# Gram-matrix transfers on GpSimd's queue from the fifth chunk on, and a later first input for the second layer

## The chip, the cores and the metric

The kernel runs on one core of a Trainium2 chip. The metric is the device time of one execution in microseconds (us). The kernel before takes 1139.2 us, the median of three runs (1139.18, 1139.20 and 1141.53).

## What is computed

A delta-rule attention over 4 batches, 8 heads, 768 steps and head size 48, whose output goes through two feed-forward layers with 3072 tokens, model width 384 and inner width 2048, all in float32:

```
for t in range(768):
    y[:, :, t] = q[t] @ state
    v_old = state^T @ k[t]                      # k normalised
    state += beta[t] * outer(k[t], v[t] - v_old)
x  = y as 3072 tokens x 384
h  = x @ w_in;   x = (max(h, 0) + alpha * min(h, 0)) @ w_out     # layer 1
h  = max(x @ w_in2, 0);   out = (h * h) @ w_out2                 # layer 2
```

## The kernel before

The delta rule is cut into 12 chunks of 64 steps (`NCH`), and each chunk into two units u = 2c and 2c + 1 of eight (batch, head) groups of 128 partitions. A chunk needs the inverse of a triangular matrix that is built from the chunk's Gram matrix (keys times keys). This early part does not depend on the state, so it runs well ahead of the steps that carry the state on:

- `early(u)` has three pieces. `keys` normalises the keys, `transp` transposes them, and `gram` (L346) multiplies them. TensorE leaves the Gram matrix in PSUM; ScalarE copies its diagonal blocks into the tile `gs` and they are stored to `gscr` (L355); the off-diagonal blocks go to the tile `go` in two f16 parts and are stored to `oscr` (L362). With a chunk's second unit the matrix is read back from `gscr` in another layout by four loads into the tile `prob` (L370): two for each half of the partitions, one of whole rows and one of the right half of the lower rows.
- `inverse(k)` works on a pair of chunks, 2k and 2k + 1. VectorE scales `prob` (L391) and eliminates column by column (L397, L398). At its end, `fin` writes the result back over `prob` in two f16 parts and stores it to `tscr` with four stores (L406). There is one `prob` buffer, so the next pair's `prob` loads wait for these stores. I call the time between one pair's last column and the next pair's first a handover.
- `both` and `steps` are the chunk's steps. They load the inverse from `tscr` into `diag` (L422) and the off-diagonal blocks from `oscr` into `cross` (L430), and multiply with them. Keys come back through `kbd` and `ktb` (L472, L478), queries and values through `qr` and `vr` (L259, L261). The output y goes to HBM, to `x1d` (L528); for most chunks it stands in the buffer `t` of the weight pool on its way.

The feed-forward layers run beside this. Layer 1 takes a tile of 256 tokens for each chunk, layer 2 a tile of 512 tokens, and each tile passes 16 blocks j of the inner width. Every product is three matmuls with values split into a high and a low part in float32r. For a block, `emit_h` makes the first product (L632, nine matmuls), ScalarE and VectorE the nonlinearity (L110 and L639 in layer 1, L641 and L642 in layer 2) and the split of the result into `gh` (L644, ScalarE) and `gl` (L645, VectorE); `emit_acc` makes the second product (L664, nine matmuls), three blocks behind in layer 1. After a tile's last block, ScalarE copies the sums of layer 1 into a buffer of the tag `xf` (L673), and they are stored to `x2d` (L675).

`load_x(n)` loads a tile's input into `xf`, and `take_x(n)` splits it: ScalarE casts it into `xh` (L569), VectorE subtracts to get `xl` (L570). Tiles n = 0 to 11 belong to layer 1, n = 12 to 17 to layer 2. A tile of layer 2 is made of two halves of 256 tokens, from two tiles of layer 1, one in `xf` of the pool `moe` (the same single buffer that L673 writes) and one in `xf` of the pool `w2p[0]`. That pool opens where the delta rule's pools close. In it, `load_w1` loads raw weights of layer 2 (L725, GpSimd's queue, three `raw` buffers), and VectorE turns them into high and low parts, twice for each block (L589 to L592, L734, L736).

What sets the order: the program puts each piece into a list at a time t, in units of a block of layer 1 (`at`, L219), and that time, less an `ahead`, becomes the priority of its instructions (`urgency`). A planner then runs the program in a model of its own, gives each engine, among the instructions that it reckons ready, the one of highest priority, and so writes each engine's order once and for all. On the chip every engine works in that order and waits where an operand is late. Transfers are issued by SyncE (SP in the profile; it does nothing else) or by GpSimd (POOL). SP has the Gram transfers, `tscr`, `diag`, `cross`, `x1d`, `xf` and `x2d`; POOL has keys, queries, values, `kscr`, `fscr`, `kbd`, `ktb`, `bt` and most raw weights. `tc.issue_after(i)` keeps the instructions under it behind the instruction i.

Of the kernel before, what the change touches and what calls it, by code (L numbers as in the profile page):

```python
# [9 lines left out]
F32 = mybir.dt.float32  # L10
# [11 lines left out]
DM, DFF = 384, 2048  # L22
CH = 64
NCH = S // CH
# [54 lines left out]
CHAIN = 4  # L79
EARLY = 3  # L80
INV = 15
WQ = 8
UR = 7
WN = 11
# [6 lines left out]
def kernel(ctx: ExitStack, tc: tile.TileContext, qT, ktok, vtok, beta, w1, w2, alpha, cmask, hmask, eye, ident, out):  # L91
# [205 lines left out]
    def early(u):  # L297
        c, s = divmod(u, 2)
        d = {}

        def keys():
            kn = kts[c][:, 8 * s:8 * s + 8]
            rb = nr[c][:, 8 * s:8 * s + 8].unsqueeze(2).to_broadcast([128, NG, D])
            (G if c > NV else V).tensor_tensor(out=kn, in0=kn, in1=rb, op=ALU.mult)
            if u == 3:
                d["loan"] = loan(2).bitcast(F16)
            kh = d["loan"][:, 0:2 * DM].rearrange("p (t g e) -> p t g e", t=2, g=NG) if u == 3 else new(erl, [128, 2, NG, D], F16, "kh") if c else uhs[s]
            split(kh, kn, 1.0, G if c in KP else V)
            d["ktb"] = d["loan"][:, 2 * DM:2 * DM + 2 * NG * HD].rearrange("p (t g e) -> p t g e", t=2, g=NG) if u == 3 else new(erl, [128, 2, NG, HD], F16, "ktbE") if c else new(stp, [128, 2, NG, HD], F16, "ktb", KB)
            spread(d["ktb"], kh, tmask, c < SPK)  # L310
            if c:
                G.dma_start(out=kscr[u], in_=d["ktb"])

        def transp():
            ktb = d["ktb"]
            if u == 3:
                t = loan(1).bitcast(F16)[0:HD]
                kbd = [t[:, 1024 * i:1024 * i + 1024].rearrange("p (g i) -> p g i", g=NG) for i in range(2)]
                kf = t[:, 2048:3072].rearrange("p (t g i) -> p t g i", t=2, g=NG)
            else:  # L320
                whole = new(erl, [HD, 2, NG, 128], F16, "kbdE") if c else new(stp, [HD, 2, NG, 128], F16, "kbd", 2)
                kbd = [whole[:, i] for i in range(2)]
                kf = new(erl, [HD, 2, NG, CH], F16, "kf") if c else new(stp, [HD, 2, NG, CH], F16, "qh", 2)
            d["kbd"] = kbd
            for i in range(2):
                ps = bank(128, CH, ebank(c))
                for g in range(NG):
                    w = wide(ktb, i, g)
                    nc.tensor.matmul(ps[0:w.shape[1], g], lhsT=w, rhs=i2, start=True, stop=True)
                ps = ps[0:HD]  # L330
                scaled(kf[:, i], ps)
                for h in range(2):
                    o, k = heads(kbd[i])[:, :, :, h], ps.rearrange("p g (b i) -> p g b i", b=2)
                    if c > EV or h:
                        scaled(o, k, fmask[h])
                    else:
                        V.tensor_scalar(out=o, in0=k, scalar1=fmask[h], scalar2=None, op0=ALU.mult)
            if c == 0:
                kept[u] = whole, d["ktb"]
            elif u == 3:  # L340
                for i in range(2):
                    G.dma_start(out=fscr[u][:, i], in_=kbd[i])
            else:
                G.dma_start(out=fscr[u], in_=whole)
            d["kf"] = kf

        def gram():
            ps = bank(tag=ebank(c))
            for g in range(NG):
                for n, (i, j) in enumerate(((0, 0), (0, 1), (1, 0))):  # L350
                    nc.tensor.matmul(ps[:, g], lhsT=d["kbd"][i][:, g], rhs=d["kf"][:, j, g], start=n == 0, stop=n == 2)  # L351
            gs = new(stp, [128, NG, CH], F32, "pf")[:, :, 0:32] if u > UR else new(moe, [128, TOK], F32, "r1", R1).rearrange("p (g i) -> p g i", g=NG)
            for b in range(2):
                scaled(gs[64 * b:64 * b + 64], ps[64 * b:64 * b + 64, :, 32 * b:32 * b + 32])
            nc.sync.dma_start(out=gscr[c][s].rearrange("g j i -> j g i"), in_=gs)  # L355
            half = first(0, s)
            if c < 2:
                go = (d["loan"][:, 2304:2816] if u == 3 else gos[:, 512 * u:512 * u + 512]).rearrange("p (g i t) -> p g i t", i=32, t=2)[half]
            else:
                go = new(erl, [128, NG, 32, 2], F16, "go")[half]  # L360
            split(go.rearrange("p g i t -> p t g i"), ps[half, :, 32 * (1 - s):32 * (1 - s) + 32], 1.0)
            nc.sync.dma_start(out=oscr[u], in_=go)  # L362
            if u % 4 == 0:
                bts[c // 2] = new(erl, [128, 2, 32], F32, "bt")
                G.dma_start(out=bts[c // 2], in_=beta[c:c + 2].rearrange("c p i -> p c i"))
            if s:
                rows = gscr[c].rearrange("s g (q j) i -> (s g q) j i", q=4)
                for e in range(2):
                    for h, a in enumerate(halves(prob)):
                        i = nc.sync.dma_start(out=a[64 * e:64 * e + 64, c % 2], in_=rows[:, 16 * h:16 * h + 16, 16 * h:])  # L370
                        probs[c] = i.ins

        return keys, transp, gram
# [5 lines left out]
    def inverse(k):  # L379

        a, x, bt = prob, inv, bts[k]
        ops = []

        def init():
            G.memset(x, 0.0)
            for e in range(2):
                scaled(x.rearrange("p c a b -> p c (a b)")[64 * e:64 * e + 64, :, e:512:34], bt[64 * e:64 * e + 64, :, e::2], 256.0)
            for h, t in enumerate(halves(a)):
                for c in range(2):
                    b = bt[:, c, 16 * h:].unsqueeze(1).to_broadcast([128, 16, 32 - 16 * h])  # L390
                    V.scalar_tensor_tensor(out=t[:, c], in0=t[:, c], scalar=0.00390625, in1=b, op0=ALU.mult, op1=ALU.mult)  # L391

        def col(j):
            m, n = j // 2 + 1, 31 - j
            t = new(erl, [128, 272], F32, "col")[:, :2 * m * n].rearrange("p (c a b) -> p c a b", c=2, a=m)
            row = halves(a)[j // 16][:, :, j % 16:j % 16 + 1, j % 16 + 1:].to_broadcast([128, 2, m, n])
            V.tensor_tensor(out=t, in0=row, in1=x[:, :, 0:m, j:j + 1].to_broadcast([128, 2, m, n]), op=ALU.mult)  # L397
            i = V.tensor_tensor(out=x[:, :, 0:m, j + 1:], in0=x[:, :, 0:m, j + 1:], in1=t, op=ALU.subtract)  # L398
            columns.setdefault(k, []).append(i.ins)

        def fin():
            for c in range(2):
                t = a[:, c, 0:512].bitcast(F16).rearrange("p (m i t) -> p m i t", m=16, t=2)
                split(t.rearrange("p m i t -> p t m i"), x[:, c], 1.0)
                for e in range(2):
                    nc.sync.dma_start(out=tscr[2 * k + c][:, e::2], in_=t[64 * e:64 * e + 64])  # L406

        ops.append(init)
        for j in range(31):
            ops.append(lambda j=j: col(j))  # L410
        ops.append(fin)
        return ops

# [137 lines left out]
    def load_x(n):  # L551

        if n < NCH:
            xf[n] = [new(moe, [128, KD, TOK], F32, "xf")]
            nc.sync.dma_start(out=xf[n][0][0:HD], in_=x1d[n][:, 0:KD])
            nc.sync.dma_start(out=xf[n][0][HD:128], in_=x1d[n][:, KD].rearrange("(m p) i -> p m i", m=KD))
        else:
            xf[n] = [new(moe, [128, KD, TOK], F32, "xf"), new(w2p[0], [128, KD, TOK], F32, "xf")]
            for h, t in enumerate(xf[n]):
                nc.sync.dma_start(out=t, in_=x2d[n - NCH][:, :, h])  # L560

    def take_x(n):
        src = xf.pop(n)
# [2 lines left out]
        for m, (xh, xl) in enumerate(xs[n]):  # L566
            for h, t in enumerate(src):
                cols = slice(TOK * h, TOK * h + TOK)
                A.copy(out=xh[:, cols], in_=t[:, m])  # L569
                (G if m in TG and n < NCH else V).tensor_tensor(out=xl[:, cols], in0=t[:, m], in1=xh[:, cols].bitcast(F32), op=ALU.subtract)  # L570


# [45 lines left out]
            A.copy(out=wl[i], in_=ps[i])  # L618


    gt, acc = {}, {}

    def emit_h(layer, t, j):
        wh, wl = (t[0] for t in wt[layer, j])
# [16 lines left out]
            A.activation(out=g, in_=ps, func=ACTF.Relu)  # L641
            A.activation(out=g, in_=g, func=ACTF.Square)  # L642
        gh, gl = (new(p, [128, w], F32R, n, LAGB + 1 if layer else GB) for n in ("gh", "gl"))
        A.copy(out=gh, in_=g)  # L644
        (V if layer or j not in GP else G).tensor_tensor(out=gl, in0=g, in1=gh.bitcast(F32), op=ALU.subtract)  # L645
        gt[layer, t, j] = gh, gl

# [62 lines left out]
    for n in range(NCH + NCH // 2):  # L710
        t = 16 * n if n < NCH else 32 * n - 16 * NCH
        at(t - 5, load_x, n)
        at(t + TT, take_x, n)
    for j in range(NF):
        at(W0T + j, load_w0, j, ahead=AW)
    end = 16 * NCH
# [120 lines left out]
```

## Time and profile before

| | |
|---|---|
| median of 3 runs | 1139.2 us |
| the profiled execution | 1140.61 us |
| its span, first to last instruction | 1138.8 us |
| TensorE matmuls busy | 1054.2 us, 93% of the span |
| VectorE, ScalarE busy | 736.5 us, 728.6 us |
| GpSimd busy | 118.7 us, 206 instructions |
| granted TensorE clock, mean | 0.975 |

All times are microseconds from the span's start, on the one core. PE is TensorE, DVE VectorE, ACT ScalarE, POOL GpSimd and SP SyncE; an engine's name with a q is its sequencer, which issues transfers. "Busy" does not count the time in which an engine waits. The granted clock is the share of TensorE's full rate (2.4 GHz) that it was allowed in a stretch; a stretch at half the rate shows as 0.5, and a mean between 0.5 and 1 is a mix of both.

### The profile page before, as it was taken

What the parts mean: (1) busy time and instruction counts of PE and PEld (TensorE: products, weight loads), DVE (VectorE), ACT (ScalarE), POOL (GpSimd) and SP (SyncE); (2) the same over time, 40 slices, a digit from 0 to 9 for tenths busy, and PEclk for the clock granted to TensorE, in tenths of its full rate; (3) what the DMA queues carried; (4) which work ended last, traced back from release to release, by engine and by line L of the source; (5) the groups of instructions that cost most, each with busy time, mean ns of one, the idle gap of its engine ahead of it and who ended that gap; (6) DMA issues with size and microseconds to landing.
All of it is one profiled execution on the core that took longest, in us unless ns stands there. A gap on an engine that the chain in (4) does not pass through costs nothing.

```text
span 1138.8 us, 25230 instructions
## 1 busy us (share of the span) xinstructions
PE 1054.2 (93%) x9952; PEld 935.1 (82%) x9952; DVE 736.5 (65%) x1904; ACT 728.6 (64%) x1583; POOL 118.7 (10%) x206
## 2 busy tenths in 40 slices
PE   2766889899999979999999989999999999999997
PEld 2434579899999979999999989988888888888886
DVE  6998789699789869988986759888312121221211
ACT  7867678777767866885566546577645454454543
POOL 5111111111111111110110001011000000000000
PEclk9988899999999989999999989999999999999999
DMA  9585457545545464464353143343101000010000
GB/s 307 121 297 124 108 138 183 128 138 138 136 115 150 137 156 114 131 164 112 80 136 87 46 131 98 94 141 109 56 1 56 0 28 28 1 56 1 28 1 28
DMA packets 162886, 116.78 MB, mean 103 GB/s; under 512 B 122032, under 2 KB 143536, under 8 KB 162768
## 3 DMA queue, kind: packets, MB, share of 16 engines
q0 software_dynamic: 16320, 67.45, 19.3%
q1 hardware_dynamic: 146448, 47.73, 17.6%
q8 instruction: 78, 1.28, 0.5%
q14 instruction: 40, 0.33, 0.1%
HBM read 75.82 MB, written 39.32 MB: 101 GB/s over the span
## 4 chain that ended last, share of the span: by engine, by line
PE 73%; issue 8%; DMA 7%; DVE 6%; ACT 4%; SPq 1%; POOL 1%; POOLq 0%; ACTq 0%; DVEq 0%
PE h L632 32%; PE acc L664 31%; PE pa L133 3%; PE pa L123 3%; PE h L612 1%; DMA prob<-gscr 1%; DMA xf<-x2d 1%; PE h L613 1%; DMA xf<-x1d 1%; DMA al<-in_alpha_dram 1%; DMA gscr<-pf 1%; DMA vr<-in_vtok_dram 1%; ACT kbdE L110 1%; PE pe L351 0%; DVE w L590 0%
## 5 line engine op out<-in xcount | busy, mean ns | idle before, releaser
L632 PE MATMUL h<-xh,w 128*128 128x256 f32 (+1 forms) x1728 | 440.1, 325 | 4.7 <-DVE r L639 3.2
L664 PE MATMUL acc<-gh,w 128*128 128x256 f32 (+1 forms) x1728 | 431.8, 323 | 6.8 <-ACT xf L673 5.5
L632 PEld LDWEIGHTS h<-xh,w 128*128 128x128 f32 x1728 | 304.2, 192 | 29.8 <-DVE r L639 4.5
L645 DVE TENSOR_TENSOR gl<-r,gh 128x256 fp32r<-128x256 f32 (+1 forms) x288 | 145.4, 507 | 277.8 <-ACT gh L644 277.5
L664 PEld LDWEIGHTS acc<-gh,w 128*128 128x128 f32 x1728 | 299.1, 192 | 30.4 <-ACT xf L673 6.3
L632 PE MATMUL h<-xl,w 128*128 128x256 f32 (+1 forms) x864 | 278.5, 322 | 0.0
L664 PE MATMUL acc<-gl,w 128*128 128x256 f32 (+1 forms) x864 | 275.2, 322 | 3.6 <-DVE gl L645 3.4
L664 PEld LDWEIGHTS acc<-gl,w 128*128 128x128 f32 x864 | 165.2, 191 | 16.5 <-DVE gl L645 4.7
L632 PEld LDWEIGHTS h<-xl,w 128*128 128x128 f32 x864 | 166.2, 192 | 11.1
L644 ACT CAST gh<-r 128x256 fp32r<-128x256 f32 (+1 forms) x288 | 136.0, 476 | 52.9 <-DVE r L639 44.9
L641 ACT ACTIVATE r<-h 128x512 f32<-128x512 f32 x96 | 57.1, 596 | 148.0 <-PE h L632 141.2
L110 ACT ACTIVATE r<-h,sgn 128x256 f32<-128x256 f32 x192 | 89.9, 472 | 61.8 <-PE h L632 56.4
L639 DVE SCALAR_TENSOR_TENSOR r<-h,bet,r 128x256 f32<-128x256 f32 x192 | 90.9, 476 | 20.8 <-ACT r L110 19.9
L398 DVE TENSOR_TENSOR inv<-inv,col 128x252 f32<-128x252 f32 (+22 forms) x186 | 63.8, 343 | 1.7
L397 DVE TENSOR_TENSOR col<-prob,inv 128x252 f32<-128x252 f32 (+22 forms) x186 | 63.5, 341 | 1.5
L642 ACT ACTIVATE r<-r 128x512 f32<-128x512 f32 x96 | 60.7, 633 | 2.6
L123 PEld LDWEIGHTS <-kbd 96*128 96x128 f16 x1104 | 38.7, 99 | 7.7 <-issue 3.2
L612 PE MATMUL h<-w,idf 128*128 128x384 f32 x64 | 35.8, 648 | 7.3 <-ACT w L618 7.3
L133 PE MATMUL pa<-ph,ubd 128*128 128x64 f16 (+1 forms) x576 | 38.7, 194 | 0.9 <-ACT ubd L110 0.9
L569 ACT CAST xh<-xf 128x256 fp32r<-128x256 f32 x72 | 25.3, 403 | 20.0 <-DMA xf<-x2d 8.5
L570 DVE TENSOR_TENSOR xl<-xf,xh 128x256 fp32r<-128x256 f32 x72 | 26.6, 420 | 15.1 <-ACT xh L569 15.1
L133 PE MATMUL pa<-qh,sbd 96*128 96x64 f16 (+1 forms) x528 | 35.3, 194 | 0.0
(176 smaller groups left out, 1392.0 us busy)
## 6 DMA issues: line engine op xcount, KB each, us to landing
raw<-in_w_dram POOLq DMA_DIRECT2D x32, 384.0 KB, 3.4
kbd<-fscr POOLq DMA_DIRECT2D x22, 384.0 KB, 4.2
ktb<-kscr POOLq DMA_DIRECT2D x22, 384.0 KB, 3.6
kscr<-ktbE POOLq DMA_DIRECT2D x21, 384.0 KB, 3.4
fscr<-kbdE POOLq DMA_DIRECT2D x21, 384.0 KB, 3.4
w<-in_w_dram POOLq DMA_DIRECT2D x8, 768.0 KB, 9.2
w<-in_w_dram SPq DMA_DIRECT2D x8, 768.0 KB, 12.2
vr<-in_vtok_dram POOLq DMA_DIRECT2D x24, 192.0 KB, 4.1
```

Source lines behind the costliest of these rows:

```text
L110: A.activation(out=out, in_=in_, func=ACTF.Copy if isinstance(scale, float) else ACTF.Identity, scale=scale)
L123: nc.tensor.matmul(ps, lhsT=w[:, i], rhs=x[:, j], start=start and n == 0, stop=stop and n == 2)
L133: nc.tensor.matmul(ps[0:w.shape[1], g], lhsT=w, rhs=x[:, j, g], start=start and n == 0, stop=stop and n == 2)
L397: V.tensor_tensor(out=t, in0=row, in1=x[:, :, 0:m, j:j + 1].to_broadcast([128, 2, m, n]), op=ALU.mult)
L398: i = V.tensor_tensor(out=x[:, :, 0:m, j + 1:], in0=x[:, :, 0:m, j + 1:], in1=t, op=ALU.subtract)
L632: nc.tensor.matmul(ps, lhsT=a[:, sl], rhs=x, start=(n == 0), stop=(n == 8))
L639: V.scalar_tensor_tensor(out=g, in0=ps, scalar=bet[:, j:j + 1], in1=g, op0=ALU.mult, op1=ALU.max)
L641: A.activation(out=g, in_=ps, func=ACTF.Relu)
L642: A.activation(out=g, in_=g, func=ACTF.Square)
L644: A.copy(out=gh, in_=g)
L645: (V if layer or j not in GP else G).tensor_tensor(out=gl, in0=g, in1=gh.bitcast(F32), op=ALU.subtract)
L664: i = nc.tensor.matmul(acc[m], lhsT=a[:, sl], rhs=g, start=(j == 0 and n == 0 and (layer == 1 or m != 1)), stop=(j == NF - 1 and n == 2), ...
```

## The change

The four kinds of Gram transfers, and the two loads of the second layer's first input (n = 12), get a choice of queue. With `GD = "gop"` and `QG = 3` the stores to `gscr` ("g") and `oscr` ("o") and the loads of `prob` ("p") are issued by GpSimd for chunks c > 3; the stores to `tscr` ("t") stay on SyncE. With `XG = 1` both halves of input 12 are loaded by GpSimd. Its first half no longer uses `xf` of `moe` but the weight pool's buffer `t`. Its cast is put into the list at t - 0.6 instead of t - 3, and each cast is held behind the cast of `gh` of block 14 (`NF - 2`) of layer 1's last tile. Inputs 13 to 17 are as before.

```
+XG = 1
+GD = "gop"
+QG = 3
...
-            nc.sync.dma_start(out=gscr[c][s].rearrange("g j i -> j g i"), in_=gs)
+            (G if c > QG and "g" in GD else nc.sync).dma_start(out=gscr[c][s].rearrange("g j i -> j g i"), in_=gs)
...
-            nc.sync.dma_start(out=oscr[u], in_=go)
+            (G if c > QG and "o" in GD else nc.sync).dma_start(out=oscr[u], in_=go)
...
-                        i = nc.sync.dma_start(out=a[64 * e:64 * e + 64, c % 2], in_=rows[:, 16 * h:16 * h + 16, 16 * h:])
+                        i = (G if c > QG and "p" in GD else nc.sync).dma_start(out=a[64 * e:64 * e + 64, c % 2], in_=rows[:, 16 * h:16 * h + 16, 16 * h:])
...
-                    nc.sync.dma_start(out=tscr[2 * k + c][:, e::2], in_=t[64 * e:64 * e + 64])
+                    (G if 2 * k > QG and "t" in GD else nc.sync).dma_start(out=tscr[2 * k + c][:, e::2], in_=t[64 * e:64 * e + 64])
...
-            xf[n] = [new(moe, [128, KD, TOK], F32, "xf"), new(w2p[0], [128, KD, TOK], F32, "xf")]
+            one = new(wpool, [128, 2 * DM], F32, "t", TB).rearrange("p (m i) -> p m i", m=KD) if n == NCH else new(moe, [128, KD, TOK], F32, "xf")
+            xf[n] = [one, new(w2p[0], [128, KD, TOK], F32, "xf")]
             for h, t in enumerate(xf[n]):
-                nc.sync.dma_start(out=t, in_=x2d[n - NCH][:, :, h])
+                (G if n == NCH and XG else nc.sync).dma_start(out=t, in_=x2d[n - NCH][:, :, h])
...
-                A.copy(out=xh[:, cols], in_=t[:, m])
+                with tc.issue_after(last[NF - 2]) if n == NCH else nullcontext():
+                    A.copy(out=xh[:, cols], in_=t[:, m])
...
-        A.copy(out=gh, in_=g)
+        i = A.copy(out=gh, in_=g)
+        if (layer, t) == (0, NCH - 1):
+            last[j] = i.ins
...
-        at(t + TT, take_x, n)
+        at(t + (TT if n != NCH else -0.6), take_x, n)
```

## Rows read from the trace of the kernel before

**Rows 1.** The page, part 1: busy us, share of span, instructions.

```profile
PE 1054.2 (93%) x9952; PEld 935.1 (82%) x9952; DVE 736.5 (65%) x1904; ACT 728.6 (64%) x1583; POOL 118.7 (10%) x206
```

**Rows 2.** Busy by long stretches: length, busy by engine, clock, DMA share, GB/s.

```profile
160.00:600.00 440.00, 422.14 (x5922) 411.21 (x5919) 377.59 (x1085) 320.60 (x762) 66.44 (x116) 0.99 0.54 136
...
800.00:1128.00 328.00, 328.00 (x1449) 271.60 (x1448) 66.86 (x112) 165.55 (x288) 0.00 (x0) 1.00 0.06 22
```

**Rows 3.** Busy by stretches of 20 us, same columns (PE PEld DVE ACT POOL).

```profile
400.00:420.00 20.00, 13.50 (x155) 12.36 (x154) 11.55 (x24) 11.52 (x27) 2.99 (x5) 0.85 0.72 156
...
660.00:680.00 20.00, 16.11 (x116) 15.90 (x115) 10.19 (x26) 9.28 (x25) 2.13 (x4) 0.83 0.47 149
...
700.00:720.00 20.00, 17.54 (x133) 16.88 (x132) 16.79 (x44) 11.60 (x30) 1.83 (x4) 0.94 0.38 119
720.00:740.00 20.00, 20.00 (x157) 19.66 (x157) 18.15 (x46) 11.05 (x26) 2.15 (x4) 0.97 0.29 81
```

**Rows 4.** Waits, 655 to 740 us: engine, line, releaser: us, times, longest.

```profile
POOL raw L725 <- DVE w L736: 34.1, 5, 16.0
POOL raw L725 <- PE acc L664: 34.0, 1, 34.0
...
ACT xh L569 <- DMA xf<-x2d: 8.5, 2, 5.0
DVE xl L570 <- ACT xh L569: 7.9, 2, 5.0
...
PE acc L664 <- ACT xf L673: 4.5, 2, 3.9
```

**Rows 5.** The chain that ended last, in order of time: start us, us, what.

```profile
662.26 6.96 DMA xf<-x2d
...
710.70 3.93 DMA xf<-x2d
```

**Rows 6.** Timelines of ACT, PE, DVE at the seam: start us, us, what.

```profile
736.38 0.41 ACT L644 CAST gh<-r 128x256 fp32r<-128x256 f32 x1 [0.59 <-DVE r L639]
...
737.82 0.40 PE L664 MATMUL acc<-gh,w 128*128 128x256 f32 x2
738.06 0.40 PE L632 MATMUL h<-xh,w 128*128 128x512 f32 x1
...
797.82 0.55 DVE L736 TENSOR_TENSOR w<-raw,w 128x384 fp32r<-128x384 f32 x1
...
798.97 0.39 PE L632 MATMUL h<-xh,w 128*128 128x512 f32 x1
```

**Rows 7.** Timeline of DVE, 660 to 685 us.

```profile
669.75 1.10 DVE L570 TENSOR_TENSOR xl<-xf,xh 128x256 fp32r<-128x256 f32 x3 [5.02 <-ACT xh L569]
```

**Rows 8.** Timeline of SP, 370 to 430 us.

```profile
405.53 1.23 SPq L370 DMA_DIRECT2D prob<-gscr  x2
...
408.07 2.69 SPq L422 DMA_DIRECT2D diag<-tscr  x4
```

**Rows 9.** Waits of DVE and of PE, 160 to 600 us.

```profile
DVE prob L391 <- DMA prob<-gscr: 16.6, 10, 3.8
...
PE pa L123 <- DMA diag<-tscr: 4.1, 1, 4.1
...
PE acc L664 <- DVE gl L645: 2.9, 2, 1.7
```

**Rows 10.** POOL's groups by line: xcount, busy us, mean ns, idle before.

```profile
L725 POOL DMA_DIRECT2D raw<-in_w_dram x32 | 17.3, 543 | 147.6 <-DVE w L736 71.3 <-DVE t L591 35.5 <-PE acc L664 34.0
...
L478 POOL DMA_DIRECT2D ktb<-kscr x22 | 12.5, 567 | 102.5 <-PE pa L133 88.5 <-PE pa L123 9.4 <-DMA ktb<-kscr 2.7
...
L365 POOL DMA_DIRECT2D bt<-in_beta_dram x6 | 4.4, 737 | 39.4 <-DVE prob L391 26.8 <-DVE col L397 12.6
```

**Rows 11.** Timelines of POOL and DVE around 580 us.

```profile
580.37 1.39 POOL L472 DMA_DIRECT2D kbd<-fscr  x1 [5.27 <-PE pa L123]
...
580.24 0.75 DVE L211 TENSOR_SCALAR ubd<-uh,hm 128x768 f16<-128x768 f16 x2
```

More of the change, by code (lines that the diff above doesn't have):

```diff
@@ L618, in load_w0 @@
             A.copy(out=wl[i], in_=ps[i])
-    gt, acc = {}, {}
+    gt, acc, last = {}, {}, {}
     def emit_h(layer, t, j):
```

## The prediction

> **What bounds the kernel now.** I read the page first, then the busy time by stretches, then the waits, and last the timelines around the places where TensorE stood idle.
>
> On the page TensorE is busy for 1054.2 of 1138.8 us [rows 1]. From 800 us on it has no idle time at all [rows 2], so nothing can be won behind that: what can be won is the idle time and the lost clock ahead of it. The change acts from the fifth chunk's Gram matrices on (after 160 us), so two places are left: the stretch from 160 to 600 us, where TensorE idles 440 - 422.1 = 17.9 us [rows 2], and the seam of the two layers between 660 and 740 us.
>
> At the seam, 660 to 680 us has 16.11 us busy at clock 0.83, 700 to 720 us has 17.54 at 0.94, and 720 to 740 us is busy throughout at 0.97 [rows 3]. TensorE's longest wait there, 3.9 us, is for the copy of layer 1's sums (L673) [rows 4]. That copy was not slow: ScalarE, which works in order, had the casts of the second layer's input ahead of it and waited 8.5 us in two pieces for their loads, and VectorE waited 7.9 us behind those casts [rows 4]. The chain shows the two loads: one landing 6.96 us after 662.26, one 3.93 us after 710.70 us [rows 5]. Nobody needs this input yet: the second layer's first matmul starts at 738.06 us [rows 6].
>
> **Part 1: the second layer's first input.** The casts of ScalarE (L569) move from both places to behind the cast of gh of block 14 of the last tile. Removed: TensorE's idle time, 3.89 + 2.46 = 6.35 us [rows 3], and the lost clock, 20 x (0.17 + 0.06 + 0.03) = 5.2 us, if the clock falls only because TensorE idled just before, as it does in both places. By TensorE alone that is 11.5 us. But the second layer's first pass also needs its weights, which VectorE converts: the last step for block 15's w_in starts at 797.82 us, and that block's first matmul at 798.97 us [rows 6], just in time. So the seam gets shorter only as far as the conversions do, and what they surely get back is VectorE's wait, 7.9 us [rows 4]. Between 7.9 and 11.5 us I take 9.0, nearer to VectorE's figure because the last block shows no slack.
>
> What it adds at the new place: gh of block 14 ends at 736.38 + 0.41 = 736.8 us [rows 6]. Three subtractions took 1.10 us with their casts running just ahead of them [rows 7]; six end some 2.5 us later, at 739.3 us, and with about 2 us of ScalarE's other work of those microseconds in between at 741.3. Cover: at 738.06 us layer 1's last four blocks still owe 36 - 2 = 34 matmuls of their second product, at 0.12 us each (two in 0.24 us, rows 6) 4.1 us, so TensorE has work until 742.1 us. Cost 0; if the last block's gl gets stuck behind the six subtractions, up to 2 us. The tie to gh is ScalarE's own order and holds up nothing else. The two loads leave SP for POOL, where they cost two issues of 0.54 us [rows 10] among the first raw weights. POOL's waits for a raw buffer behind the conversions come to 34.1 us at the whole seam, 16.0 at the longest [rows 4], and the input has from 662 to 737 us: 0. The buffer t that the first half now uses was last used for chunk 11's y, which is out before. SP loses two issues and a wait that nobody stood behind: 0.
>
> **Part 2: the Gram matrices' stores and loads.** Per chunk, eight issues (two gscr, two oscr, four prob) leave SP; tscr, diag, cross, x1d and the first layer's xf stay. Where SP's queue shows: ahead of the chunk that starts near 410 us, SP issues two prob, one gscr and one oscr from 405.53 us on and reaches the diag loads at 408.07 us [rows 8]; TensorE waits 4.1 us for diag, once [rows 9]. Without the four, diag goes out 2.54 us sooner: -2.5 us. In the other three handovers from one pair's inverse to the next TensorE shows no wait for diag, so 0 there. The clock lost around this stall is 20 x 0.15 = 3.0 us [rows 3]; some 4 of the 6.5 us of idle time in that window stay, so I count half, -1.5.
>
> What POOL pays: a load of 128 runs (raw) issues in 543 ns, one of 256 runs (bt) in 737 ns [rows 10]; 194 ns for 128 runs make 1.90 us for 1024 runs, an estimate from these two rows. The gscr stores and two of a chunk's four prob loads have 1024 runs; the other two prob loads and the oscr stores have 64. That is 4 x 1.90 + 4 x 0.54 = 9.8 us a chunk and 78 us over eight chunks, on an engine that is busy for a tenth of the span: room enough. But the four prob loads then need 4.9 us to issue, against 4 x 0.62 = 2.5 us on SP [rows 8]; the inverse starts 2.4 us later. VectorE, which scales prob in order, waited 16.6 us for these loads between 160 and 600 us, and TensorE lost 2.9 us waiting for gl [rows 9]: 0.17 us per us. Eight times 2.4 us more of VectorE's waiting costs 3.4 us at that rate. From below: the loads no longer queue behind SP's x1d and diag, and if all these waits went, -2.9 us. I take +2.2, nearer to the upper end, as the added issue time is sure and the saved queueing is not. Part 2: -2.5 - 1.5 + 2.2 = -1.8 us.
>
> One POOL load, at 580.37 us, took 1.39 us to issue where the raw loads take 0.54, beside VectorE's f16 products from 580.24 us on [rows 10, 11]. The Trainium skill, SBUF — State Buffer, section "Who interferes with whom", says that a transfer issued by GpSimd stalls while VectorE runs an operation in a mode that takes the port they share. By that rule, and this row agrees, a moved issue that meets such a product costs 0.9 us more, and the sum comes out by a few us higher the more of them meet one.
>
> **The sum.** -9.0 - 1.8 = -10.8 us. The profiled execution took 1140.61 us for a span of 1138.8, 1.4 above the median of the three runs, 1139.2; off the median that gives 1128.4 us.
>
> **The rivals.**
> - *The handovers come free altogether.* POOL issues the prob loads as soon as their buffer is free, not behind SP's stores. For it: VectorE's 16.6 us of waits for prob all lie in those crowded windows [rows 9]. Then the whole of part 1 (11.5) comes and 4.1 + 2.9 + 3.0 = 10.0 us of part 2: 1117.7 us. Against it: 1.90 us an issue. Chance 0.20.
> - *The weights hold the seam.* TensorE gains its 11.5 us before 740 us and gives most of it back waiting for converted blocks. For it: the 1.2 us between 797.82 and 798.97; against it: VectorE gets 7.9 us back. With 2 us left of each part 1135 us, with nothing left 1139. Chance 0.13, of which 0.04 within 0.2%.
> - *Slower: POOL's queue holds the Gram loads.* POOL works in order and mostly waits: before its 22 ktb loads it stood 102.5 us, 4.7 us each [rows 10]. If a Gram store or a prob load stands behind such a wait at each of the four handovers, the inverse, and with it the end of the delta rule, comes 4 x 4.7 = 18.6 us later. The second layer's weight loads wait for that end (POOL stood 34.0 us before the first of them, rows 4), and the conversions have no slack: 1139.2 - 9 + 18.6 = 1148.8 us. It decides from some 3.3 us a handover on (9 + 4 us to eat up, over four). Against it: the planner puts each POOL instruction where it reckons it ready. VectorE's hold on the shared port would add to the same delay and has its chance in here. Chance 0.17.
> - *Nothing comes of it.* The planner lays all queues out anew, and part 2 costs what part 1 gives: 1139 us. Chance 0.04. That part 1 is not in force can hardly be, as the casts are tied to gh of block 14.
>
> **How the numbers follow.** The forecast has 0.46, with a range of its own from 1122 to 1134 us (part 1 between 11.5 and 7.9 less 2, part 2 between -6 and +1). A measurement of this kernel tells about 0.2%, 2.3 us, from no change. Faster: 0.46 + 0.20 + 0.09 = 0.75; within: 0.04 + 0.04 = 0.08; slower: 0.17. The range from 1115 to 1143 takes in the forecast, the free handovers, the held seam and no change; it leaves out the held POOL queue and gains beyond both sums.
>
> **What would show it.** Right in part 1: no wait of ScalarE for xf<-x2d between 655 and 720 us, no idle time of TensorE there and clock 1.00; the casts L569 right behind the last tile's gh of block 14; TensorE busy across the seam. Right in part 2: no SP issue of prob, gscr or oscr from the fifth chunk on, POOL issues of some 1.9 us, the wait for diag near 1.5 us or gone. Wrong in part 1: new waits of L632 for w or xl after 735 us. Wrong in part 2: POOL issues of 3 us and more, longer waits of VectorE for prob, and a first raw load later than 662 us.

## The result, and the profile after

The changed kernel takes 1129.57 us (median of four runs, 1125.12 to 1134.56), the kernel before in the same comparison 1140.37 us (four runs, 1139.18 to 1147.23). The ratio is 0.9879, 95% interval [0.9843, 0.9915]: faster by 1.2%. (The plain quotient of the two medians, 0.9905, lies inside.) The forecast of 1128.4 us is met within 1.2 us. As a difference, 10.8 us were forecast; the medians differ by 10.8 us, and by the ratio the gain is 13.8 us (9.7 to 17.9) of 1139.2. The profiled run of the changed kernel took 1130.09 us for a span of 1128.3. The diff moves the line numbers by 3 to 7: L632 is now L637, L664 L671, L673 L680, L569 L574, L391 L394.

The page, part 1:

```profile
PE 1054.8 (93%) x9952; PEld 935.8 (83%) x9952; DVE 736.3 (65%) x1904; ACT 729.3 (65%) x1583; POOL 167.9 (15%) x272
```

TensorE's work is the same as in [rows 1], 1054.8 us; GpSimd has 66 instructions more, the 64 Gram transfers and the two loads. Now the busy time by stretches, first four stretches of the kernel before that I had not shown (columns as in rows 2):

```profile
200.00:220.00 20.00, 16.75 (x227) 15.86 (x226) 11.33 (x25) 15.86 (x40) 2.14 (x4) 0.98 0.56 127
220.00:240.00 20.00, 20.00 (x299) 19.64 (x299) 19.11 (x68) 12.77 (x32) 3.08 (x5) 0.93 0.40 112
420.00:440.00 20.00, 19.85 (x269) 19.18 (x269) 17.63 (x62) 14.04 (x36) 2.90 (x5) 0.98 0.47 114
500.00:520.00 20.00, 19.57 (x202) 18.99 (x198) 12.81 (x32) 12.74 (x31) 1.47 (x2) 1.00 0.71 136
```

And the same view of the changed kernel:

```profile
160.00:600.00 440.00, 427.47 (x5973) 417.14 (x5973) 379.74 (x1091) 324.83 (x766) 113.80 (x181) 0.98 0.52 136
200.00:220.00 20.00, 15.24 (x170) 14.36 (x168) 9.79 (x22) 12.40 (x30) 4.00 (x7) 0.83 0.45 125
400.00:420.00 20.00, 19.55 (x234) 19.25 (x234) 13.96 (x32) 14.34 (x37) 7.79 (x12) 1.00 0.65 132
420.00:440.00 20.00, 18.17 (x242) 17.62 (x242) 16.95 (x61) 12.84 (x32) 2.98 (x6) 0.91 0.38 93
500.00:520.00 20.00, 17.88 (x172) 17.60 (x172) 11.88 (x29) 13.87 (x34) 8.39 (x12) 0.91 0.57 116
660.00:680.00 20.00, 19.13 (x154) 18.36 (x153) 14.03 (x37) 10.54 (x26) 4.38 (x8) 1.00 0.59 188
700.00:720.00 20.00, 20.00 (x169) 20.00 (x168) 19.02 (x48) 11.94 (x29) 2.72 (x5) 1.00 0.46 135
720.00:740.00 20.00, 20.00 (x131) 18.30 (x131) 18.90 (x47) 15.34 (x37) 2.79 (x5) 1.00 0.34 101
```

Against [rows 3]: at the seam TensorE is busy for 3.02 + 2.46 = 5.5 us more, and the clock is full in all three stretches, worth the 5.2 us that were lost there. The stall near 410 us is smaller and comes later: from 400 to 420 us 13.50 us busy at 0.85 became 19.55 at 1.00, but from 420 to 440 us 19.85 at 0.98 became 18.17 at 0.91. Together that is 4.4 us of idle time and 1.6 us of clock won.

In two other places the changed kernel lost. Near 200 us the kernel before already stalled (16.75 us busy at 0.98, then 20.00 at 0.93); now it is 15.24 at 0.83, then 20.00 at 1.00, which is 1.5 us more idle time and 1.6 us more lost to the clock. From 500 to 520 us it is 1.7 and 1.8 us more. Over 160 to 600 us the idle time fell from 17.9 us [rows 2] to 440 - 427.47 = 12.5, while the clock fell from 0.99 to 0.98.

The waits of TensorE and of VectorE from 160 to 600 us (two answers):

```profile
PE h L637 <- ACT xh L574: 4.6, 1, 4.6
PE pa L126 <- DMA diag<-tscr: 3.8, 3, 2.1
...
DVE prob L394 <- DMA prob<-gscr: 5.5, 4, 2.4
```

VectorE's waits for `prob` fell from 16.6 us in ten pieces to 5.5 in four [rows 9]. The one wait of 4.1 us for `diag` became three of 2.1 at most, the longest of them at 515 us. New is the first line: 4.6 us for the split input of a tile of layer 1. The timelines of SP and of ACT show what it is:

```profile
193.94 2.21 SPq L425 DMA_DIRECT2D diag<-tscr  x4
196.20 0.58 SPq L531 DMA_DIRECT2D x1d<-t  x1
...
201.65 0.70 SPq L559 DMA_DIRECT2D xf<-x1d  x1
...
206.06 1.02 ACT L574 CAST xh<-xf 128x256 fp32r<-128x256 f32 x3 [4.63 <-DMA xf<-x1d]
```

The output y of a chunk is stored (`x1d`) behind four `diag` loads, read back as the tile's input some five microseconds later, and ScalarE stands 4.63 us for it, TensorE behind it.

At the seam, the timelines of ACT (first and last of the six casts) and of DVE (the last step for block 15's w_in, the last weight conversion but one):

```profile
725.57 0.71 ACT L649 CAST gh<-r 128x256 fp32r<-128x256 f32 x2
726.18 0.41 ACT L574 CAST xh<-t 128x256 fp32r<-128x256 f32 x1
...
727.71 0.41 ACT L574 CAST xh<-xf 128x256 fp32r<-128x256 f32 x1
...
785.96 0.55 DVE L743 TENSOR_TENSOR w<-raw,w 128x384 fp32r<-128x384 f32 x1
```

The casts stand right behind `gh` of block 14 and wait for nothing. This step starts at 785.96 us instead of 797.82 [rows 6], 11.9 us sooner, and that block's first matmul at 787.95 us instead of 798.97. TensorE shows no wait at all between 735 and 800 us, as it showed none in the kernel before.

POOL's groups by line (count, busy us, mean ns, idle before):

```profile
L373 POOL DMA_DIRECT2D prob<-gscr x32 | 21.7, 685 | 18.6 <-DMA tscr<-prob 6.5 <-issue 4.4 <-DMA gscr<-pf 3.1
...
L358 POOL DMA_DIRECT2D gscr<-pf x16 | 14.8, 926 | 25.5 <-ACT pf L113 25.5
L365 POOL DMA_DIRECT2D oscr<-go x16 | 8.9, 554 | 4.6 <-DVE go L120 3.2 <-DVE r L251 0.8 <-DVE col L400 0.3
```

A `gscr` store of 1024 runs takes 926 ns to issue, where I had reckoned 1.90 us, and the `prob` loads, half of them of 1024 runs, 685 ns on the mean.

### The profile page after: what moved, and what is told of

Read it like the earlier page. It is cut to its first block, busy times and chain, and to the rows that moved or that the text cites. A ratio compares the mean times of both kernels' runs of the same rounds, so it can differ in the third digit from the quotient of the medians.

```text
span 1128.3 us, 25262 instructions
## 1 busy us (share of the span) xinstructions
PE 1054.8 (93%) x9952; PEld 935.8 (83%) x9952; DVE 736.3 (65%) x1904; ACT 729.3 (65%) x1583; POOL 167.9 (15%) x272
## 3 DMA queue, kind: packets, MB, share of 16 engines
q0 software_dynamic: 19104, 74.53, 22.1%
q1 hardware_dynamic: 109808, 40.65, 14.4%
## 4 chain that ended last, share of the span: by engine, by line
PE 72%; DMA 8%; issue 7%; ACT 6%; DVE 5%; SPq 1%; POOL 1%; POOLq 0%; DVEq 0%; ACTq 0%
PE h L637 31%; PE acc L671 31%; PE pa L136 3%; PE pa L126 3%; DMA diag<-tscr 1%; ACT kbdE L113 1%; PE h L617 1%; PE h L618 1%; DMA prob<-gscr 1%; DMA xf<-x1d 1%; DMA raw<-in_w_dram 1%; DMA al<-in_alpha_dram 1%; SPq L425 1%; DMA vr<-in_vtok_dram 1%; DMA tscr<-prob 1%
## 5 line engine op out<-in xcount | busy, mean ns | idle before, releaser
L637 PE MATMUL h<-xh,w 128*128 128x256 f32 (+1 forms) x1728 | 440.6, 325 | 5.6 <-ACT xh L574 4.6
L671 PE MATMUL acc<-gh,w 128*128 128x256 f32 (+1 forms) x1728 | 433.2, 322 | 1.3 <-ACT xf L680 1.0
L637 PEld LDWEIGHTS h<-xh,w 128*128 128x128 f32 x1728 | 304.7, 192 | 30.2 <-ACT xh L574 4.7
L671 PEld LDWEIGHTS acc<-gh,w 128*128 128x128 f32 x1728 | 300.2, 191 | 26.6 <-ACT xf L680 1.6
L637 PE MATMUL h<-xl,w 128*128 128x256 f32 (+1 forms) x864 | 278.8, 323 | 0.0
L671 PE MATMUL acc<-gl,w 128*128 128x256 f32 (+1 forms) x864 | 276.2, 323 | 1.4 <-DVE gl L652 1.4
L671 PEld LDWEIGHTS acc<-gl,w 128*128 128x128 f32 x864 | 165.2, 191 | 13.8 <-DVE gl L652 2.3
L637 PEld LDWEIGHTS h<-xl,w 128*128 128x128 f32 x864 | 166.6, 193 | 11.2
L732 POOL DMA_DIRECT2D raw<-in_w_dram x32 | 17.7, 553 | 135.7 <-DVE w L743 84.3
L126 PE MATMUL pa<-qh,kbd 96*128 96x64 f16 x576 | 32.5, 198 | 2.5 <-DVE qh L122 1.0
## 6 DMA issues: line engine op xcount, KB each, us to landing
w<-in_w_dram SPq DMA_DIRECT2D x8, 768.0 KB, 11.9
```

The source lines that it names most:

```text
L126: nc.tensor.matmul(ps, lhsT=w[:, i], rhs=x[:, j], start=start and n == 0, stop=stop and n == 2)
L637: nc.tensor.matmul(ps, lhsT=a[:, sl], rhs=x, start=(n == 0), stop=(n == 8))
L671: i = nc.tensor.matmul(acc[m], lhsT=a[:, sl], rhs=g, start=(j == 0 and n == 0 and (layer == 1 or m != 1)), stop=(j == NF - 1 and n == 2), ...
```

## The experiments

Eleven kernels, one of them in two batches; three batches, each on another chip and with its own runs of the kernel before. Each kernel was timed six times, but the late input alone seven, the Gram transfers alone twelve and the repeat of the loads five times (medians of the kernel before 1143.46, 1143.25 and 1145.08 us). Diffs are against the changed kernel. The quoted expectations were written before each run.

### The two parts, each alone

**Late input alone** (Gram transfers back on SyncE):

```
-GD = "gop"
+GD = ""
```

> The late, moved first input of the second layer alone; all Gram transfers stay on SyncE. Theory (two separate gains, the seam's of some 9 to 10 us and the handovers' of 0 to 3 us): ratio to before 0.990 to 0.993, 1128 to 1131 us; between 655 and 720 us no wait of ScalarE for xf<-x2d, TensorE idle for at most 1.5 us where it was 6.35, clock 1.00; the stall near 410 us with its wait of some 4 us for diag stays as before. Rival (the gain is the handovers'): 0.998 to 1.000, the seam's idle time comes back behind 740 us as waits for weights.

1132.24 us, ratio 0.9915 [0.9881, 0.9949]. Busy by stretches:

```profile
400.00:420.00 20.00, 12.65 (x171) 11.54 (x168) 12.59 (x29) 13.17 (x32) 2.44 (x4) 0.86 0.65 143
660.00:800.00 140.00, 138.63 (x922) 126.55 (x921) 120.09 (x286) 91.15 (x202) 19.32 (x34) 1.00 0.41 121
```

The seam is as in the changed kernel, the stall near 410 us as in the kernel before. 0.85% of 1139.2 us are 9.7 us (5.8 to 13.6): near the term of 9.0.

**Gram transfers alone** (first input early, on SyncE, in `xf` of `moe`):

```
-XG = 1
+XG = 0
...
-            one = new(wpool, [128, 2 * DM], F32, "t", TB).rearrange("p (m i) -> p m i", m=KD) if n == NCH else new(moe, [128, KD, TOK], F32, "xf")
+            one = new(moe, [128, KD, TOK], F32, "xf")
...
-                with tc.issue_after(last[NF - 2]) if n == NCH else nullcontext():
+                with nullcontext():
...
-        at(t + (TT if n != NCH else -0.6), take_x, n)
+        at(t + TT, take_x, n)
```

> The Gram transfers on GpSimd alone; the second layer's first input as before (SyncE, early cast, buffer xf). Theory (two separate gains): ratio to before 0.996 to 1.000; VectorE's waits for prob between 160 and 600 us fall from 16.6 to some 5 us, the wait for diag near 410 us goes, and one or two new stalls appear; the seam keeps its two waits of ScalarE for xf<-x2d (8 us together) and a clock under 0.95. Rival (the gain is the handovers'): 0.990 to 0.993.

1139.72 us, ratio 0.9957 [0.993, 0.9984]. Busy by stretches:

```profile
200.00:220.00 20.00, 14.87 (x192) 14.27 (x193) 9.14 (x21) 12.52 (x31) 3.76 (x7) 0.83 0.43 108
400.00:420.00 20.00, 18.88 (x228) 18.54 (x228) 14.54 (x35) 13.40 (x36) 8.56 (x14) 1.00 0.69 152
660.00:680.00 20.00, 15.89 (x121) 15.69 (x120) 13.69 (x35) 9.66 (x25) 1.07 (x2) 0.91 0.52 162
```

The seam's stall is back, most of the one near 410 us is gone, and the loss near 200 us is there: it belongs to the Gram transfers. 0.43% are 4.9 us (1.8 to 8.0); the 1.8 of my sum is the end of that interval, so that it was too small is likely but not sure. The parts add up: 0.9915 x 0.9957 = 0.9872, against 0.9879 for both. (The plain quotients of the medians are 0.9902 and 0.9967, 11.2 and 3.7 us.)

One more thing can be read here. From 700 to 720 us TensorE is busy for 17.54 us, just as in the kernel before [rows 3], but the granted clock is 1.00 there and in the next 20 us, and not 0.94 and 0.97: the same idle time does not always cost clock.

### What in part 1 does it: the time of the cast, the buffer, the queue

**Late cast alone** (loads on SyncE into `xf` of `moe`; cast late, behind `gh` of block 14):

```
-XG = 1
-GD = "gop"
+XG = 0
+GD = ""
...
-            one = new(wpool, [128, 2 * DM], F32, "t", TB).rearrange("p (m i) -> p m i", m=KD) if n == NCH else new(moe, [128, KD, TOK], F32, "xf")
+            one = new(moe, [128, KD, TOK], F32, "xf")
```

> Only the cast of the second layer's first input is late; its loads stay on SyncE and its first half stays in the buffer xf that layer 1's sums use too. Gram transfers as before. Theory (ScalarE stood with the cast in front of its other work; where the loads come from does not matter): as with buffer and queue moved too, 0.990 to 0.993, no stall of TensorE between 660 and 720 us. Rival (the shared buffer counts: the copy of the last sums waits for the late cast): a new wait of L673's successor line for xf and a ratio of 0.995 to 1.000.

1131.07 us, ratio 0.9897 [0.9861, 0.9933]: the whole gain of part 1. The timeline of ACT has the six casts in one go and the copies of the last tile behind them without a wait:

```profile
727.87 1.94 ACT L574 CAST xh<-xf 128x256 fp32r<-128x256 f32 x6
735.08 0.38 ACT L680 COPY xf<-acc 128x256 f32<-128x256 f32 x1
```

The shared buffer is free in time, so another buffer and another queue are not needed beside a late cast.

**Buffer and queue alone** (cast as early as before):

```
-GD = "gop"
+GD = ""
...
-                with tc.issue_after(last[NF - 2]) if n == NCH else nullcontext():
+                with nullcontext():
...
-        at(t + (TT if n != NCH else -0.6), take_x, n)
+        at(t + TT, take_x, n)
```

> Only the loads of the second layer's first input move (GpSimd's queue, buffer t); its cast stays early. Gram transfers as before. Theory: the second stall (2.5 us at 705 to 717) goes, since its load no longer waits for the store of layer 1's sums, but the first (3.9 us at 667) stays, since ScalarE still meets a load just issued: ratio 0.995 to 0.998. Rival (the loads are the cause): both stalls go, 0.990 to 0.993.

1133.17 us, ratio 0.9912 [0.9877, 0.9946]: I had expected the first stall to stay, and it went but for 1.7 us (18.33 us busy from 660 to 680 us, clock 1.00). So the last batch took the buffer and the queue apart, each with the edits of this run besides.

**Queue alone** (loads on GpSimd, into `xf` of `moe`):

```
-            one = new(wpool, [128, 2 * DM], F32, "t", TB).rearrange("p (m i) -> p m i", m=KD) if n == NCH else new(moe, [128, KD, TOK], F32, "xf")
+            one = new(moe, [128, KD, TOK], F32, "xf")
```

> The second layer's first input on GpSimd's queue, but in xf of moe and cast as early as before; Gram transfers on SyncE as before. Theory (the queue does it: on SyncE the two loads stand behind stores that wait, on GpSimd's queue they go out and land before the casts' turn): ScalarE's waits for xf<-x2d between 655 and 720 us fall from 8.5 to 2 us or less, TensorE shows no gap over 1 us at the seam, ratio 0.990 to 0.993. Rival (the buffer does it: xf of moe is free only once layer 1's copy of sums is stored, so a load into it is late on any queue): the waits stay near 8 us, gaps near 3.9 and 2.4 us, ratio 0.997 to 1.000.

**Buffer alone** (loads on SyncE, the first half into `t`):

```
-XG = 1
+XG = 0
```

> The second layer's first input in the weight pool's buffer t, but still loaded by SyncE and cast as early as before; Gram transfers on SyncE as before. Theory (the queue does it): ScalarE still waits 4 us or more for xf<-x2d, TensorE keeps a gap of 2 us or more at the seam, ratio 0.995 to 1.000. Rival (the buffer does it): no gap over 1 us at the seam, ratio 0.990 to 0.993.

Queue alone: 1136.35 us, ratio 0.9911 [0.9883, 0.9939], the whole gain, though ScalarE still waits 2.7 us in two pieces. Buffer alone: 1137.27 us, 0.993 [0.9906, 0.9955]: a gap as the first theory had it, but a ratio at the end of the second one's range. The intervals overlap, so the two times by themselves do not tell the buffer from the queue. ScalarE's order around 660 to 676 us does; here is its timeline in the kernel before:

```profile
663.22 0.72 ACT L673 COPY xf<-acc 128x256 f32<-128x256 f32 x2
669.32 1.02 ACT L569 CAST xh<-xf 128x256 fp32r<-128x256 f32 x3 [5.04 <-DMA xf<-x2d]
670.61 0.36 ACT L673 COPY xf<-acc 128x256 f32<-128x256 f32 x1
```

with the buffer alone:

```profile
665.15 0.72 ACT L680 COPY xf<-acc 128x256 f32<-128x256 f32 x2
671.42 1.02 ACT L574 CAST xh<-xf 128x256 fp32r<-128x256 f32 x3 [5.21 <-DMA xf<-x2d]
672.72 0.36 ACT L680 COPY xf<-acc 128x256 f32<-128x256 f32 x1
```

with the queue alone:

```profile
668.93 0.72 ACT L680 COPY xf<-acc 128x256 f32<-128x256 f32 x2
672.87 0.37 ACT L680 COPY xf<-acc 128x256 f32<-128x256 f32 x1
674.89 1.02 ACT L574 CAST xh<-xf 128x256 fp32r<-128x256 f32 x3 [0.53 <-DMA xf<-x2d]
```

and with both:

```profile
664.11 0.72 ACT L680 COPY xf<-acc 128x256 f32<-128x256 f32 x2
668.37 0.37 ACT L680 COPY xf<-acc 128x256 f32<-128x256 f32 x1
670.47 1.02 ACT L574 CAST xh<-xf 128x256 fp32r<-128x256 f32 x3 [0.60 <-DMA xf<-x2d]
```

Where the first casts stand between the second and the third copy of the sums, ScalarE waits some 5 us for the load, and the third copy, for which TensorE waits, is late. On GpSimd's queue the load was no quicker: with the queue alone it was issued at 668.99 us and its cast began at 674.89, 5.9 us later (6.96 us to land in rows 5). What changed is the order that the planner wrote: the third copy ahead of the casts. My theory's reason, loads that go out sooner, was wrong even where its numbers came true. The buffer alone leaves this order and its gap (4.07 us of TensorE's time at 669 us), and takes away only the second one, near 710 us: that half is now loaded into `t` and cast at 674.52 us.

### What in part 2 does it

**Loads of `prob` alone**, and later **the same program again**:

```
-GD = "gop"
+GD = "p"
```

> The changed kernel with only the prob loads on GpSimd; gscr and oscr stores stay on SyncE. Theory (SyncE's queue in front of diag and the prob loads' own wait count; the stores are small change): ratio to before 0.986 to 0.990; the wait for diag near 410 us falls from 4.1 to under 2 us, VectorE's waits for prob between 160 and 600 us to under 8 us (16.6 before). Rival (the stores are as much of it): prob waits over 12 us, ratio as with the late input alone, 0.9915 or more.

> The same program as the run with the loads alone (0.9824), once more beside the others. Theory (it beats the whole change): ratio 0.979 to 0.986. Rival (the first measurement was a lucky one): ratio 0.986 to 0.990.

1124.49 us, ratio 0.9824 [0.9786, 0.9862], and again 1122.51 us, 0.9799 [0.9772, 0.9826]. Both are below the whole change (0.9879), in the second run with intervals apart: this version beats both kernels. From the second one's stretches, SP's and ACT's timelines and the waits of 160 to 600 us:

```profile
160.00:600.00 440.00, 429.81 (x6064) 420.03 (x6063) 386.50 (x1106) 329.78 (x779) 88.28 (x150) 1.00 0.53 138
200.00:220.00 20.00, 18.34 (x262) 17.23 (x260) 12.67 (x27) 17.36 (x42) 3.71 (x7) 1.00 0.73 187
220.00:240.00 20.00, 18.09 (x229) 17.78 (x229) 18.77 (x64) 12.91 (x31) 5.85 (x9) 0.91 0.41 113
...
193.87 0.58 SPq L531 DMA_DIRECT2D x1d<-t  x1
201.46 0.43 SPq L559 DMA_DIRECT2D xf<-x1d  x1
...
205.94 1.02 ACT L574 CAST xh<-xf 128x256 fp32r<-128x256 f32 x3
...
PE pa L126 <- DMA diag<-tscr: 2.9, 2, 2.4
...
DVE prob L394 <- DMA prob<-gscr: 5.4, 8, 1.9
```

VectorE's wait for `prob` is as short as in the changed kernel (5.4 against 5.5 us; in the first run's profile it is 8.6, a little over the 8 that I had expected), so it is the loads that shorten it. Near 200 us TensorE loses what it lost in the kernel before: from 200 to 240 us it is busy for 36.43 us (36.75 before), and the clock costs 1.8 us in both. The longer stall of the changed kernel, its wait for the input, is absent. It isn't the order of `x1d` and `diag` that makes the difference: `x1d` goes out 2.3 us sooner here, but the input is loaded and cast at the same time (205.94 against 206.06 us). ScalarE and TensorE simply have other work ahead of it in this plan.

This is not why the loads alone are faster than the whole change, though. ScalarE begins to copy the sums of layer 1's fifth tile at 413.55 us here (412.88 in the first run) and at 412.59 us in the changed kernel; for the tenth tile it is 656.54 us (658.75) and 661.27. The difference arises behind 410 us, where the changed kernel's stalls at 420 to 440 and 500 to 520 us are smaller or absent (20.00 and 19.85 us busy here at clock 1.00).

**Stores alone** (`gscr` and `oscr`):

```
-GD = "gop"
+GD = "go"
```

> The changed kernel with only the gscr and oscr stores on GpSimd; prob loads stay on SyncE. Theory (the loads count): ratio 0.990 to 0.993, VectorE's waits for prob stay near 16 us and the wait for diag near 410 us at 3 us or more. Rival (the stores count): 0.986 to 0.989 and both waits halved.

1132.92 us, ratio 0.9919 [0.9887, 0.995], the same as the late input alone: no gain of the stores' move by itself can be told. VectorE's waits for `prob` hardly fall:

```profile
DVE prob L394 <- DMA prob<-gscr: 14.0, 7, 3.3
```

The profile puts 6.4 us more of VectorE's waits at `prob` down to `diag` loads. I had expected TensorE to keep a wait of 3 us or more for `diag` near 410 us, and that was wrong: there are three waits from 160 to 600 us, of 1.8 us at most. The time did not get shorter by it.

**All four kinds**, the stores to `tscr` too:

```
-GD = "gop"
+GD = "gopt"
```

> The changed kernel with the tscr stores on GpSimd too (chunks 4 on). Theory (SyncE's order in front of diag and x1d is what is left): SyncE issues four transfers fewer per handover, but diag still waits for the tscr stores to land, so the waits for diag stay at 3 to 5 us in all: ratio 0.985 to 0.991. Rival (GpSimd's queue is full at the handovers): tscr stands behind prob or kbd there, diag waits grow over 8 us, ratio over 0.993.

1130.92 us, ratio 0.9897 [0.9863, 0.993], no better than the change. Near 200 us it has the stall again: 14.39 us busy at clock 0.83 from 200 to 220 us. The waits for `diag` are one of 1.9 us, less than the 3 to 5 us that I had expected.

**The change from the seventh chunk on:**

```
-QG = 3
+QG = 5
```

> The changed kernel with the Gram transfers on GpSimd only from the seventh chunk on, so that the handover near 200 us is SyncE's again. Theory (the new stall of 4.6 us near 202 us, where x1d stands behind diag on SyncE and layer 1's input is late, belongs to that handover's new order): no stall over 3 us there and the clock of 200 to 220 us back near 0.98; the stall near 410 us stays small; ratio 0.980 to 0.986. Rival (the planner's order near 200 us is chance, any other will do the same): a stall of like size somewhere else between 160 and 330 us, ratio 0.987 to 0.990.

1128.48 us, ratio 0.987 [0.9832, 0.9908]. Near 200 us the stall costs less than in the kernel before (3.5 us idle from 200 to 240 us and no clock), and the time is that of the changed kernel all the same, within the intervals. A stall stands elsewhere instead, from 300 to 320 us, where the changed kernel has 18.73 us busy at 1.00:

```profile
200.00:220.00 20.00, 17.25 (x239) 16.30 (x236) 10.67 (x23) 16.33 (x42) 2.14 (x4) 1.00 0.58 128
300.00:320.00 20.00, 17.07 (x182) 16.49 (x181) 11.18 (x25) 10.32 (x26) 7.70 (x12) 0.91 0.51 92
```

The copy of the first tile's sums is 8.8 us ahead of the changed kernel's (209.51 against 218.31 us), that of the third 1.8 us behind (316.49 against 314.65). Place and ratio are those of the second theory: a new order moves the stall.

**Loads alone, from the seventh chunk on:**

```
-GD = "gop"
-QG = 3
+GD = "p"
+QG = 5
```

> The late input as in the change; of the Gram transfers only the loads of prob on GpSimd's queue, and from the seventh chunk on. Theory (the loads alone carry part 2, and the stall near 200 us comes from the fifth and sixth chunk's): no TensorE gap over 2 us between 195 and 225 us, ratio 0.980 to 0.984, a little below the loads from the fifth chunk on. Rival (the plan differs anew with each edit and the gains of the Gram transfers are of that size): ratio 0.984 to 0.990, with a stall of 2 us or more in another place between 160 and 600 us.

1134.92 us, ratio 0.9909 [0.988, 0.9937]: above both theories, no better than the late input alone. There is no stall over 2 us near 200 us, as the first theory had it, but from 160 to 600 us the busy time is 423.79 us, 3.6 and 6.0 us below the two runs of the loads from the fifth chunk on (427.41 and 429.81). TensorE stops for `diag` at 316 us, the stall in another place that the second theory asked for (timeline of PE):

```profile
316.15 0.76 PE L126 MATMUL pa<-rhl,diag 128*128 128x48 f16 x24 [2.21 <-DMA diag<-tscr]
```

So avoiding the stall near 200 us by sparing the fifth and sixth chunk is not what makes the loads alone fast. Which of those two chunks' loads, or which piece of the new plan, is worth the 1.1% between these two versions stays open. With it stays open how much of part 2's gain is the queue's and how much is that of a plan that happened to come out well: the same move two chunks later gains nothing that can be told beside the late input.

## Why the prediction was right

**Part 1, -9.0 us: right in size and place.** The late input alone gives -9.7 us (-13.6 to -5.8). At the seam 5.5 us of idle time and 5.2 us of clock came back, all but 0.9 us of the 11.5. That the clock had fallen only because TensorE idled held: with the idle time gone it is 1.00 in all three stretches. But idle time need not lower it, as the Gram transfers alone show: 17.54 us busy at 1.00 from 700 to 720 us. The new place of the casts costs nothing, as reckoned. The weights were the reason for taking 9.0 and not 11.5. With the late input alone, the last step for block 15's w_in starts at 788.66 us, 9.2 us sooner than before [rows 6], not much more than VectorE's 7.9, and that block's first matmul at 790.24 us, 8.7 us sooner. No wait for a weight shows; whether they would have held TensorE back had they come later was not tried. I also took buffer, queue and late cast as one edit. The runs show that the late cast alone does it, that the queue alone does it too, by the order it leads the planner to, and that the buffer alone takes away one of the two gaps.

**Part 2, -1.8 us: right in sign, perhaps too small, with one term of the wrong sign.** The Gram transfers alone give -4.9 us (-8.0 to -1.8).

- The term that failed is "POOL's issue price", +2.2. The 1.90 us for 1024 runs came from a straight line through 128 and 256 runs; 926 ns were measured. Four `prob` loads take 4 x 0.685 = 2.7 us on POOL, 0.2 more than the 2.5 on SP, not 2.4 more. With the price gone, the saved queueing decided, and VectorE's waits for `prob` fell by 11.1 us. At my own rate of 0.17 us per us that is -1.9; in place of +2.2 the sum becomes -2.5 - 1.5 - 1.9 = -5.9 us, of which stalls that it doesn't have take a part back.
- The `diag` term, -2.5 - 1.5, was too small where it stood and too large as a whole: from 400 to 440 us 4.4 us of idle time and 1.6 us of clock came back, but `diag` is still waited for, 3.8 us in three places. The one at 515 us stands in the stretch from 500 to 520 us, which lost 1.7 us of busy time and 1.8 us of clock.
- Not foreseen: the wait for the input near 200 us, 1.5 us more idle time and 1.6 us more of lost clock than before from 200 to 240 us. I had asked what waits behind the moved transfers on GpSimd's queue and not what a new plan of all the engines does elsewhere.

**The hit within 1.2 us is in part luck.** Errors made up for each other. By these figures the sum charged 2.2 + 1.9 = 4.1 us too much for POOL's issues and counted 2.0 us too little from 400 to 440 us, but it lacks the 3.1 us lost near 200 us and the 3.5 us lost near 510 us.

**The rivals.** The slower one, POOL's queue holding the Gram loads, fell: POOL stood 25.5 us before the 16 stores and 18.6 us before the 32 loads, and yet VectorE waited less, and the first raw load went out at 659.73 us, not after 662. The weights did not hold the seam. The free handovers did not come with the whole change. With the loads alone their time came: 0.9824 and 0.9799 of 1139.2 are 1119.2 and 1116.3 us, and this rival gave 1117.7. Their mechanism came only in part, as waits for `diag` of 2.9 us and for `prob` of 5.4 us stay.

**The shared port.** None of the 64 moved Gram issues took as long as the one of 1.39 us did beside VectorE's products [rows 11]: the longest took 0.95 us (`gscr`), 0.87 us (`prob`) and 0.56 us (`oscr`). By the rule of the Trainium skill, SBUF — State Buffer, section "Who interferes with whom", the sum would have come out higher for each that met such a product. The changed kernel's trace shows no case of it.

## What to carry to other kernels

An early cast of an input that nobody needs yet can hold an in-order engine for microseconds, and cost nearly as much again in TensorE's clock (here 6.35 us of idle time and 5.2 us of clock); tie such an instruction behind the work that must not wait. When transfers are moved off a crowded queue, move the loads that somebody waits for and try the stores separately: here the loads from the fifth chunk on were worth about 1% and the stores nothing that could be told. Where a planner orders every engine, an edit of a queue is also an edit of all the orders, so compare the orders before crediting the queue.

## What the runs showed of the hardware

Two things I had not expected. GpSimd's issue time grew little with the number of runs: 554 ns for 64 runs (`oscr`), 926 ns for 1024 (`gscr`). And the same transfers are fewer packets on its queue: by the shapes, 34,816 runs of the Gram transfers and 768 of the two input loads left SyncE's queue, which shows 36,640 packets less (146448 to 109808), while GpSimd's shows only 2,784 more (16320 to 19104), for the same 7.1 MB. The page, part 3, of the changed kernel (packets, MB, share; q0 is GpSimd's, q1 SyncE's):

```profile
q0 software_dynamic: 19104, 74.53, 22.1%
q1 hardware_dynamic: 109808, 40.65, 14.4%
```

The granted clock also differs between runs of one program. The four runs of the changed kernel have spans of 1123.2, 1127.1, 1128.3 and 1132.5 us at mean clocks of 0.982, 0.978, 0.975 and 0.971: over the 9.3 us between the ends, 0.011 x 1128 = 12.4 us of clock, so the clock can account for the whole spread. Whether it is the cause, or falls where TensorE idles more, is not shown.
